# Attention blocks of a fused attention and two-layer MLP kernel: the values of one block and the scores of the next issued as one run of TensorE into two shared PSUM banks

## The chip, the cores and the metric

The kernel runs on one core of a Trainium2 chip. The metric is the device time of one execution in microseconds (us). The kernel before took 1147.94 us in the median of three runs (1147.36 to 1148.22). The profile is of one further execution.

## What is computed

The reference has three parts in a chain. The first is chunked attention: every chunk of 32 queries sees 8 memory keys, 16 tokens to the left, its own 32 and 8 to the right, 64 keys in the middle of a sequence. The other two are MLP layers on 3072 tokens, with a model width of 512 and a hidden width of 2048.

```python
# attention: batch 4, 8 heads, 768 tokens, head size 64; for every chunk of 32 queries
k_full = concatenate([mem_k, k_ctx], axis=2)
scores = scale * matmul(q_c, k_full.transpose(0, 1, 3, 2))
scores = scores - max(scores, axis=-1, keepdims=True)
a = exp(scores)
a = a / (sum(a, axis=-1, keepdims=True) + 1e-09)
out[:, :, c_start:c_end] = matmul(a, v_full)
# layer 1
h = x @ w_in
x = maximum(0.01 * h, h) @ w_out
# layer 2
h = x @ w_in2
P = a[0] + a[1]*h + a[2]*h**2 + a[3]*h**3
Q = 1 + abs(b[0])*abs(h) + abs(b[1])*h**2
out = (P / (Q + 1e-6)) @ w_out2
```

## The kernel before

The MLP layers are cut into 6 tiles of 512 tokens, and each tile into 16 steps `c` over the hidden width. A step has 12 matmuls of 128x512 for the hidden values (`emit_h`, PSUM tile `hps`) and 12 for the sum over the hidden width (`emit_y` in layer 1, `emit_o` in layer 2, PSUM tiles `acc`). `emit_h` runs two steps ahead in layer 1. Between the two groups of a step, and behind the second, there are gaps, numbered 2c and 2c+1, in which other work is put; `wide(slot)` calls what the table `wide_at` holds for that gap. Gaps are places in the program's order and not times: each engine works through its own list and waits for semaphores.

Attention for the first two tiles is computed before, in small ("narrow") blocks. For the other four tiles it is computed in 16 "wide" blocks of 128 tokens, numbered 8 to 23, while the matmuls of layer 1 run. `wide_plan` says in which gap each part of block j stands. Its scores stand in gap u = at[j], which is 28, 35 and 42 for blocks 8 to 10, 49 for block 11, and 8 more for each later block. The parts are:

- `wide_load_qk`, `wide_load_v`: loads of q and k by SyncE's DMA queue (SP), of v by GpSimd's (POOL).
- `wide_q`, `wide_k` (VectorE): transposes of 32x32 pieces, then a write to a DRAM buffer (`park_dram`); `wide_qk` reads that back with rows and columns rearranged. A block thus turns its q (tile `qT`) and k (tile `pb`) by a trip through DRAM.
- `wide_s`: the scores, 32 matmuls on 64x32 pieces of the array (64 rows, 32 columns) into two PSUM banks (tile `pss`), then on VectorE the row maximum and its subtraction (lines 634 and 635), which move the scores to the SBUF tile `t`.
- `wide_e` (ScalarE): exp. `wide_n` (VectorE): sum, reciprocal, product.
- `wide_p` (VectorE): transposes to tile `pm`, then a write to DRAM (line 546); `turn_in(2, ...)` reads it back in four parts (line 553).
- `wide_x`: the values, 32 matmuls on 64x64 pieces into two more PSUM banks (tile `psx`), then a copy on ScalarE (line 675) and a subtraction on VectorE (line 676) that make the two parts of the layer's input.

The pool `psw` has four PSUM banks, shared in turn by `hps`, `pss` and `psx`. `stage` puts the preparation of layer 2's weights into the same gaps: a load of 512 KB (line 227), a ScalarE scaling, three VectorE operations (lines 246 to 249) and a store (line 272). SyncE's queue issues its DMAs in program order, so a DMA that waits for its data holds up those behind it. An fp32 matmul of the small kind stands in the trace as two.

Of the kernel before, what the change touches and what calls it, by code (L numbers as in the profile page):

```python
# [9 lines left out]
F32 = mybir.dt.float32  # L10
# [6 lines left out]
P = 128  # L17
# [7 lines left out]
def kernel(  # L25
# [507 lines left out]
    PW = WIN // 2  # L533
    MP = NM // 2
    WPS = S // P
    wq, wqT, wm = {}, {}, {}
    v_mem, k_mem = [None], [None]
    kw = kall.rearrange("p n h d -> p (n h d)")
    kwT = pall.rearrange("p n c e h m -> p (n c e h m)")
    vw = vall.rearrange("p n h d -> p (n h d)").rearrange("p (c h d) -> p c h d", c=NCH, h=H // 2)  # L540
# [7 lines left out]
    def turn_in(n, j, dst):  # L548

        d = dst.rearrange("p (c w) -> p c w", c=NCH)  # L550
        s = park[n][j % 2].rearrange("(c p) (g w) -> g p c w", c=NCH, g=4)
        for g in range(4):
            nc.sync.dma_start(out=d[g * 32:(g + 1) * 32], in_=s[g])
# [57 lines left out]
    def wide_qk(j):  # L611
        turn_in(0, j, wqT[j])
        turn_in(1, j, kwT)

    def wide_s(j):
        blk = j % WPS
        qt = wqT.pop(j).rearrange("p (c n m) -> p c n m", c=NCH, n=NP)
        kt = kwT.rearrange("p (c n m) -> p c n m", c=NCH, n=NP)
        ps = [psw.tile([P, 512], F32, tag="ps", name="pss")[:, :NP * WIN].rearrange("p (n m) -> p n m", n=NP)
              for e in range(2)]  # L620
        for p in range(NP):
            for e in range(2):
                r = slice(e * 64, e * 64 + 64)
                for c in range(NCH):
                    nc.tensor.matmul(ps[e][c * CHUNK:(c + 1) * CHUNK, p, :], qt[r, c, p, :], kt[r, c, p, :],  # L625
                                     start=True, stop=True)
        mx = tmp.tile([P, 2, NP, 1], F32, tag="mx", name="mx")
        t = tmp.tile([P, 2, NP, WIN], F32, tag="P", name="t", bufs=3)
        for e in range(2):
            if blk == 0:  # L630
                nc.vector.memset(ps[e][0:CHUNK, :, NM:NM + LCTX], NEG)
            if blk == WPS - 1:
                nc.vector.memset(ps[e][P - CHUNK:P, :, WIN - RCTX:WIN], NEG)
            nc.vector.tensor_reduce(out=mx[:, e], in_=ps[e], op=ALU.max, axis=AX.X, negate=True)
            nc.vector.tensor_tensor(out=t[:, e], in0=ps[e], in1=mx[:, e].to_broadcast([P, NP, WIN]), op=ALU.add)
        wm[j] = t
# [20 lines left out]

    def wide_x(j):
        pt = pwT.rearrange("p (c h m) -> p c h m", c=NCH, h=4)
        ps = [psw.tile([P, 512], F32, tag="ps", name="psx")[:, :2 * P].rearrange("p (i m) -> p i m", i=2)  # L660
              for hh in range(2)]
        for i in range(2):
            for c in range(NCH):
                for hh in range(2):
                    r = slice(hh * WIN, hh * WIN + WIN)
                    for e in range(2):
                        nc.tensor.matmul(ps[hh][e * 64:e * 64 + 64, i, c * CHUNK:(c + 1) * CHUNK],  # L667
                                         vw[r, c, 2 * i + e, :], pt[r, c, 2 * i + e, :], start=True, stop=True)
        n, o = divmod(j * P, NMAX)
        if n not in xt:  # L670
            xt[n] = (xpool.tile([P, KC, NMAX], F32R, tag="xh", name="xh"),
                     xpool.tile([P, KC, NMAX], F32R, tag="xl", name="xl"))
        for hh in range(2):
            xh, xl = (x[:, 2 * hh:2 * hh + 2, o:o + P] for x in xt[n])
            nc.scalar.copy(out=xh, in_=ps[hh])
            nc.vector.tensor_tensor(out=xl, in0=ps[hh], in1=xh.bitcast(F32), op=ALU.subtract)
# [5 lines left out]
    def wide_plan():  # L682
        def put(slot, *fns):
            wide_at.setdefault(slot, []).extend(fns)
        n0 = WIDE_FROM * NMAX // P
        last = NT // P - 1
        TB = NMAX // P
        base = 2 * FC * (WIDE_FROM - 1)
        at = {j: base - 7 + 8 * (j - n0) for j in range(n0, last + 1)}
        at[n0], at[n0 + 1], at[n0 + 2] = base - 4, base + 3, base + 10  # L690
        put(at[n0] - 7, lambda: wide_load_qk(n0))
        put(at[n0] - 5, lambda: wide_q(n0), lambda: wide_k(n0))
        put(at[n0] - 4, lambda: wide_qk(n0), lambda: wide_load_qk(n0 + 1))
        for j in range(n0, last + 1):
            u = at[j]
            put(u, lambda j=j: wide_s(j))
            put(u + 1, lambda j=j: wide_e(j))
            if j < last:
                put(u + 1, lambda j=j: wide_q(j + 1))
                put(u + 2, lambda j=j: wide_k(j + 1))  # L700
                put(u + 3, lambda j=j: wide_qk(j + 1))
            put(u + 3, lambda j=j: wide_n(j), lambda j=j: wide_load_v(j))
            put(u + 4, lambda j=j: wide_p(j))
            put(u + 5, lambda j=j: turn_in(2, j, pwT))
            put(u + 6, lambda j=j: wide_load_qk(j + 2))
            put(u + (9 if j % TB == TB - 1 else 10), lambda j=j: wide_x(j))

    def wide(slot):
        for fn in wide_at.get(slot, ()):
# [383 lines left out]
```

## Time and profile before

| | |
|---|---|
| median of three runs | 1147.94 us |
| profiled execution, its time | 1148.0 us |
| its span, first to last instruction | 1146.2 us |
| TensorE matmul busy | 1131.7 us (99%) |
| VectorE, ScalarE, GpSimd busy | 67%, 55%, 20% |
| chain that ended last | TensorE 95%, VectorE 3% |
| wide values and wide scores, share of that chain | 2% and 1% |
| TensorE's waits from 136 to 530 us, where the wide blocks are | 0.4 us |

The span begins with the first instruction and ends with the last; the 1.8 us between it and the profiled execution's time lie outside. Busy time of TensorE is the union of its matmul records, which overlap since matmuls are pipelined: a record of a 128x512 matmul lasts 0.39 us, and the next begins 0.23 us after it. Costs on TensorE are therefore read from starts, not from durations. In the rows of a timeline equal instructions that follow each other are merged, with their number at the end, and a bracket gives idle time and who ended it. A row of the DMA queue of SyncE (SPq) says when DMAs were issued and not when they landed.

### The profile page before, as it was taken

The page shows a single profiled execution, that of the slowest core. Times are in us where ns is not written, and L with a number is a line of the kernel's source. Part 1 is how long each engine was busy: PE and PEld are TensorE (multiplying, and loading weights), DVE is VectorE, ACT ScalarE, POOL GpSimd, SP SyncE. Part 2 cuts the span into 40 slices and gives each one's busy share as a digit, 9 for nine tenths or more (in the row PEclk, how much of TensorE's full clock was granted, in tenths as well). Part 3 has the DMA queues.
Part 4 walks back from the last instruction along what each step waited for, and adds up shares of the span by engine and source line. Part 5 has one row for each costly group of instructions (what it writes and reads, how often), then busy time and mean ns, then how long its engine had stood idle before and what let it go on. Part 6 is the DMA issues. An engine that isn't in the chain of part 4 may idle for free.

```text
span 1146.2 us, 19651 instructions
## 1 busy us (share of the span) xinstructions
PE 1131.7 (99%) x7616; PEld 928.3 (81%) x7616; DVE 769.7 (67%) x1318; ACT 631.8 (55%) x1149; POOL 232.1 (20%) x264
## 2 busy tenths in 40 slices
PE   7999999999999999999999999999999999999998
PEld 6777788888888888888888888888888888888886
DVE  5887846555565555542345886887887888788775
ACT  4677632232232223223346876776777777777765
POOL 3000302231221322210000222222222222222222
PEclk9999999999999999999999999999999999999999
DMA  9966687797778777742342101001100100100101
GB/s 187 260 178 196 187 226 206 213 251 206 202 215 241 208 196 230 207 142 98 97 133 83 65 1 47 28 1 39 36 1 29 46 1 15 59 1 1 37 1 37
DMA packets 148472, 131.98 MB, mean 115 GB/s; under 512 B 63296, under 2 KB 118944, under 8 KB 148380
## 3 DMA queue, kind: packets, MB, share of 16 engines
q1 hardware_dynamic: 143372, 123.25, 37.6%
q0 software_dynamic: 4864, 7.45, 2.8%
q8 instruction: 60, 0.98, 0.4%
q14 instruction: 32, 0.26, 0.1%
q10 hardware_dynamic: 144, 0.03, 0.0%
HBM read 92.92 MB, written 37.75 MB: 114 GB/s over the span
## 4 chain that ended last, share of the span: by engine, by line
PE 95%; DVE 3%; ACT 1%; issue 1%; POOL 0%; DVEq 0%; POOLq 0%
PE hps L753 45%; PE acc L849 23%; PE acc L811 22%; PE psx L667 2%; PE pss L625 1%; PE pss L460 1%; PE hot L867 1%; DVE wwall L178 1%; PE psx L444 0%; PE psx L514 0%; DVE wwall L180 0%; PE psk L378 0%; DVE wwall L177 0%; ACT w L188 0%; DVE w L194 0%
## 5 line engine op out<-in xcount | busy, mean ns | idle before, releaser
L811 PE MATMUL acc<-g,w 128*128 128x512 f32 x1152 | 278.7, 391 | 0.1
L849 PE MATMUL acc<-w,g 128*128 128x512 f32 x1152 | 275.4, 389 | 0.0
L849 PEld LDWEIGHTS acc<-w,g 128*128 128x128 f32 x1152 | 216.2, 188 | 44.8
L811 PEld LDWEIGHTS acc<-g,w 128*128 128x128 f32 x1152 | 214.7, 188 | 46.1 <-ACT w L188 0.5
L763 ACT ACTIVATE g<-hps 128x512 fp32r<-128x512 f32 x96 | 57.4, 598 | 307.1 <-PE hps L753 307.1
L789 POOL TENSOR_TENSOR g<-R,g 128x512 fp32r<-128x512 f32 x96 | 124.2, 1294 | 504.4 <-ACT g L788 466.1
L753 PE MATMUL hps<-xh,w 128*128 128x512 f32 x768 | 209.0, 395 | 3.8 <-ACT pm L484 1.5
L753 PE MATMUL hps<-yh,w 128*128 128x512 f32 x768 | 204.1, 389 | 0.0
L766 DVE TENSOR_TENSOR g<-s,g 128x512 fp32r<-128x512 f32 x96 | 66.2, 690 | 177.6 <-ACT s L764 174.4
L753 PEld LDWEIGHTS hps<-xh,w 128*128 128x128 f32 x768 | 141.2, 188 | 34.6 <-ACT w L188 2.0
L753 PEld LDWEIGHTS hps<-yh,w 128*128 128x128 f32 x768 | 144.3, 188 | 29.9
L590 POOL DMA_DIRECT2D vb<-in_v_dram x128 | 83.2, 651 | 260.5 <-PE psx L667 207.9
L776 ACT ACTIVATE A<-hps 128x512 f32<-128x512 f32 x96 | 57.2, 596 | 113.9 <-PE hps L753 113.9
L792 DVE SCALAR_TENSOR_TENSOR A<-A,small,pb 128x512 f32<-128x512 f32 x96 | 72.0, 750 | 56.2 <-ACT pb L777 56.2
L753 PE MATMUL hps<-xl,w 128*128 128x512 f32 x384 | 103.0, 390 | 0.0
L753 PE MATMUL hps<-yl,w 128*128 128x512 f32 x384 | 102.6, 389 | 0.0
L783 DVE SCALAR_TENSOR_TENSOR A<-A,pb 128x512 f32<-128x512 f32 x96 | 66.5, 692 | 30.2 <-ACT pb L796 30.2
L753 PEld LDWEIGHTS hps<-xl,w 128*128 128x128 f32 x384 | 72.1, 188 | 15.7
L753 PEld LDWEIGHTS hps<-yl,w 128*128 128x128 f32 x384 | 72.1, 188 | 14.9
L778 ACT ACTIVATE R<-hps,small 128x512 f32<-128x512 f32 x96 | 75.0, 781 | 0.0
L785 DVE SCALAR_TENSOR_TENSOR R<-R,small,A 128x512 f32<-128x512 f32 x96 | 72.2, 752 | 3.4
L794 DVE SCALAR_TENSOR_TENSOR R<-R,small,hps 128x512 f32<-128x512 f32 x96 | 71.8, 748 | 3.4
(112 smaller groups left out, 1140.1 us busy)
## 6 DMA issues: line engine op xcount, KB each, us to landing
wr<-in_moe_w_in_dram SPq DMA_DIRECT2D x32, 512.0 KB
wr<-in_moe_w_out_dram SPq DMA_DIRECT2D x32, 512.0 KB
park_dram<-pb SPq DMA_DIRECT2D x16, 512.0 KB
pb<-park_dram SPq DMA_DIRECT2D x64, 128.0 KB
w_dram<-wwall SPq DMA_DIRECT2D x32, 256.0 KB
wb<-w_dram SPq DMA_DIRECT2D x32, 256.0 KB
kb<-in_k_dram SPq DMA_DIRECT2D x59, 112.0 KB
vb<-in_v_dram POOLq DMA_DIRECT2D x118, 56.0 KB, 3.3
```

The costliest lines, as they stand in the source:

```text
L590: nc.gpsimd.dma_start(out=vw[r + at:r + at + n, c], in_=v[bi, hs, lo:lo + n, :].rearrange("h p d -> p h d"))
L753: nc.tensor.matmul(ps[:, :n], w_[:, ws], x_[:, kk, :], start=(kk == 0 and m == 0), stop=(kk == KC - 1 and m == 2))
L763: nc.scalar.activation(out=gh, in_=ps, func=AF.Prelu, alpha=0.01)
L766: return [lambda: nc.vector.tensor_tensor(out=gl, in0=s, in1=gh.bitcast(F32), op=ALU.subtract)]
L778: nc.scalar.activation(out=R, in_=ps, func=AF.Identity, scale=ncf[:, 3:4], bias=ncf[:, 2:3])
L783: nc.vector.scalar_tensor_tensor(out=A0, in0=A0, scalar=ONE, in1=U0, op0=ALU.add, op1=ALU.mult)
L785: nc.vector.scalar_tensor_tensor(out=R0, in0=R0, scalar=ncf[:, 0:1], in1=A0, op0=ALU.add, op1=ALU.mult)
L789: nc.gpsimd.tensor_tensor(out=gl, in0=R0, in1=gh.bitcast(F32), op=ALU.subtract)
L792: nc.vector.scalar_tensor_tensor(out=A, in0=A, scalar=babs[:, 1:2], in1=U, op0=ALU.mult, op1=ALU.add)
L794: nc.vector.scalar_tensor_tensor(out=R, in0=R, scalar=ncf[:, 1:2], in1=ps, op0=ALU.add, op1=ALU.mult)
L811: nc.tensor.matmul(acc[i][d][:, :n], w_[:, ws], g_, start=(f == 0 and m == 0), stop=(f == FC - 1 and m == 2))
L849: nc.tensor.matmul(acc[i][s], g_[:, ss], w_, start=(f == 0 and m == 0), stop=(f == FC - 1 and m == 2))
```

## The change

Values of block j-1 and scores of block j are issued in one gap, u of block j: first the 32 value matmuls, then the 32 score matmuls, then VectorE's maximum and subtraction of the scores (now a function of its own, `wide_m`), and then the copy and subtraction of the values (`wide_y`). Both write to the same two PSUM banks, taken by `wide_banks` for the whole run: the scores to columns 0 to 255 of a bank, the values to columns 256 to 511. Values of block j thus stand in gap u+8 (u+7 for blocks 8 to 10), where they stood in u+10 or u+9. Normalisation, transposes with their write to DRAM, and the read back move up by a gap each, from u+3, u+4 and u+5 to u+2, u+3 and u+4, and the load of v from u+3 to u+2.

```diff
+    def wide_banks():
+        banks[:] = [psw.tile([P, 512], F32, tag="ps", name="run") for _ in range(2)]
+
     def wide_s(j):
         ...
-        ps = [psw.tile([P, 512], F32, tag="ps", name="pss")[:, :NP * WIN].rearrange("p (n m) -> p n m", n=NP)
-              for e in range(2)]
+        ps = [t[:, :NP * WIN].rearrange("p (n m) -> p n m", n=NP) for t in banks]
         ...
+        wm[j] = ps
+
+    def wide_m(j):
+        blk = j % WPS
+        ps = wm[j]
         ...
     def wide_x(j):
         pt = pwT.rearrange("p (c h m) -> p c h m", c=NCH, h=4)
-        ps = [psw.tile([P, 512], F32, tag="ps", name="psx")[:, :2 * P].rearrange("p (i m) -> p i m", i=2)
-              for hh in range(2)]
+        ps = [t[:, 512 - 2 * P:].rearrange("p (i m) -> p i m", i=2) for t in banks]
         ...
+        wx[j] = ps
+
+    def wide_y(j):
+        ps = wx.pop(j)
         ...
             u = at[j]
-            put(u, lambda j=j: wide_s(j))
+            if j > n0:
+                put(u, wide_banks, lambda j=j: wide_x(j - 1), lambda j=j: wide_s(j),
+                    lambda j=j: wide_m(j), lambda j=j: wide_y(j - 1))
+            else:
+                put(u, wide_banks, lambda j=j: wide_s(j), lambda j=j: wide_m(j))
             put(u + 1, lambda j=j: wide_e(j))
             ...
-            put(u + 3, lambda j=j: wide_n(j), lambda j=j: wide_load_v(j))
-            put(u + 4, lambda j=j: wide_p(j))
-            put(u + 5, lambda j=j: turn_in(2, j, pwT))
+            put(u + 2, lambda j=j: wide_n(j), lambda j=j: wide_load_v(j))
+            put(u + 3, lambda j=j: wide_p(j))
+            put(u + 4, lambda j=j: turn_in(2, j, pwT))
             put(u + 6, lambda j=j: wide_load_qk(j + 2))
-            put(u + (9 if j % TB == TB - 1 else 10), lambda j=j: wide_x(j))
+        put(at[last] + 8, wide_banks, lambda: wide_x(last), lambda: wide_y(last))
```

TensorE before, from the last matmuls ahead of the scores of block 10 to behind the values of block 9. The scores are line 625 and the values line 667.

```order
L753 MATMUL hps<-xh,w 128x512 x4
L625 MATMUL pss<-pb,qT 32x64 x32
L811 MATMUL acc<-g,w 128x512 x12
L753 MATMUL hps<-xh,w 128x512 x4
L753 MATMUL hps<-xl,w 128x512 x4
L753 MATMUL hps<-xh,w 128x512 x4
L811 MATMUL acc<-g,w 128x512 x12
L667 MATMUL psx<-pm,vb 64x32 x32
L753 MATMUL hps<-xh,w 128x512 x4
```

TensorE now, at the same place. Lines 674 and 628 are the values and the scores, 768 and 826 are what 753 and 811 were.

```order
L768 MATMUL hps<-xh,w 128x512 x4
L674 MATMUL run<-pm,vb 64x32 x32
L628 MATMUL run<-pb,qT 32x64 x32
L826 MATMUL acc<-g,w 128x512 x12
L768 MATMUL hps<-xh,w 128x512 x4
L768 MATMUL hps<-xl,w 128x512 x4
L768 MATMUL hps<-xh,w 128x512 x4
L826 MATMUL acc<-g,w 128x512 x12
L768 MATMUL hps<-xh,w 128x512 x4
```

The values of block 9 moved from 36 big matmuls behind the scores of block 10 to directly ahead of them.

VectorE before, in the same block 10, from the transposes of k of block 11 (line 608) to the transposes to `pm` (line 655); line 676 belongs to the values of block 9, lines 644 to 647 are the normalisation, 246 to 249 the weights.

```order
L608 STREAM_TRANSPOSE pb<-kb 128x4x2x32 x4
L676 TENSOR_TENSOR xl<-psx,xh 128x2x128 x2
L644 TENSOR_REDUCE sm<-t 128x8
L645 TENSOR_SCALAR sm<-sm 128x8
L646 RECIPROCAL sm<-sm 128x8
L647 TENSOR_TENSOR t<-t,sm 128x512
L246 TENSOR_SCALAR wwall<-wwall 128x512
L247 SCALAR_TENSOR_TENSOR wwall<-wr,wwall 128x512
L249 SCALAR_TENSOR_TENSOR wwall<-wr,wwall 128x512
L766 TENSOR_TENSOR g<-s,g 128x512
L655 STREAM_TRANSPOSE pm<-t 128x2x2x32 x4
```

VectorE now, at that place (609, 652 to 655 and 663 are what 608, 644 to 647 and 655 were).

```order
L609 STREAM_TRANSPOSE pb<-kb 128x4x2x32 x4
L652 TENSOR_REDUCE sm<-t 128x8
L653 TENSOR_SCALAR sm<-sm 128x8
L654 RECIPROCAL sm<-sm 128x8
L655 TENSOR_TENSOR t<-t,sm 128x512
L663 STREAM_TRANSPOSE pm<-t 128x2x2x32 x4
L246 TENSOR_SCALAR wwall<-wwall 128x512
```

The subtraction of the values is gone from here, and the transposes to `pm` stand ahead of the weights' operations and of one `g`.

SyncE's DMA queue before, block 10: the trip of q and k of block 11 and of `pm` of block 10 through DRAM.

```order
L546 DMA park_dram<-pb 128x1024
L553 DMA qT<-park_dram 32x4x128 x4
L553 DMA pb<-park_dram 32x4x256 x4
L227 DMA wr<-in_moe_w_out_dram 128x1024
L546 DMA park_dram<-pm 128x512
L272 DMA w_dram<-wwall 128x512
L553 DMA pm<-park_dram 32x4x128 x4
```

The same place of the queue now.

```order
L547 DMA park_dram<-pb 128x1024
L554 DMA qT<-park_dram 32x4x128 x4
L554 DMA pb<-park_dram 32x4x256 x4
L547 DMA park_dram<-pm 128x512
L227 DMA wr<-in_moe_w_out_dram 128x1024
L554 DMA pm<-park_dram 32x4x128 x4
L272 DMA w_dram<-wwall 128x512
```

The write of `pm` went ahead of the 512 KB load, and its read back ahead of the weights' store.

## Rows read from the trace of the kernel before

**Rows 1.** Busy time 136 to 530 us: length, engines (count), granted clock, DMA share, GB/s.
```profile
136.00:530.00 394.00, 393.64 (x3618) 320.20 (x3617) 214.35 (x489) 117.74 (x228) 87.83 (x138) 1.00 0.74 206
```

**Rows 2.** Chain of waits, its last long piece: start us, length us, what.
```profile
1131.24 10.89 PE acc L849 x48
```

**Rows 3.** Timeline of TensorE, 182 to 199 us: start us, length us, instruction, count.
```profile
185.89 0.86 PE L625 MATMUL pss<-pb,qT 64*32 64x64 f32 x64
186.68 3.02 PE L811 MATMUL acc<-g,w 128*128 128x512 f32 x12
...
192.25 2.88 PE L811 MATMUL acc<-g,w 128*128 128x512 f32 x12
195.07 1.14 PE L667 MATMUL psx<-pm,vb 64*64 64x32 f32 x64
```

**Rows 4.** Groups by line and shape: count, busy us, mean ns, idle before.
```profile
L625 PE MATMUL pss<-pb,qT 64*32 64x64 f32 x1024 | 13.9, 224 | 0.0
```

**Rows 5.** Timeline of TensorE, narrow blocks, 70 and 119 us.
```profile
70.92 0.38 PE L502 MATMUL pst<-ident,pm 128*128 128x128 f32 x2
71.24 0.65 PE L460 MATMUL pss<-kT,qT 64*32 64x64 f32 x32
...
119.16 0.38 PE L502 MATMUL pst<-ident,pm 128*128 128x128 f32 x2
119.30 3.01 PE L811 MATMUL acc<-g,w 128*128 128x512 f32 x12
```

**Rows 6.** Timeline of TensorE: scores of blocks 8, 9, 11, 12 and 13.
```profile
144.07 1.00 PE L625 MATMUL pss<-pb,qT 64*32 64x64 f32 x64
...
164.27 0.86 PE L625 MATMUL pss<-pb,qT 64*32 64x64 f32 x64
...
207.24 0.86 PE L625 MATMUL pss<-pb,qT 64*32 64x64 f32 x64
...
231.31 0.86 PE L625 MATMUL pss<-pb,qT 64*32 64x64 f32 x64
...
255.37 0.86 PE L625 MATMUL pss<-pb,qT 64*32 64x64 f32 x64
```

**Rows 7.** Timeline of SyncE's DMA queue (issues), block 8.
```profile
156.47 1.80 SPq L553 DMA_DIRECT2D pb<-park_dram  x4
158.85 0.69 SPq L546 DMA_DIRECT2D park_dram<-pm  x1
161.95 1.73 SPq L553 DMA_DIRECT2D pm<-park_dram  x4
```

**Rows 8.** The same queue, block 9.
```profile
176.91 3.58 SPq L553 DMA_DIRECT2D pb<-park_dram  x4
...
181.10 0.38 SPq L546 DMA_DIRECT2D park_dram<-pm  x1
185.31 1.74 SPq L553 DMA_DIRECT2D pm<-park_dram  x4
```

**Rows 9.** The same queue, block 10.
```profile
195.88 0.32 SPq L546 DMA_DIRECT2D park_dram<-pb  x1
...
201.05 1.73 SPq L553 DMA_DIRECT2D pb<-park_dram  x4
...
203.36 0.38 SPq L546 DMA_DIRECT2D park_dram<-pm  x1
...
209.72 1.82 SPq L553 DMA_DIRECT2D pm<-park_dram  x4
```

**Rows 10.** The same queue, block 13.
```profile
274.48 1.75 SPq L553 DMA_DIRECT2D pm<-park_dram  x4
```

**Rows 11.** The same queue, block 23, when little else is moved.
```profile
511.64 0.32 SPq L546 DMA_DIRECT2D park_dram<-pm  x1
...
513.74 1.74 SPq L553 DMA_DIRECT2D pm<-park_dram  x4
```

**Rows 12.** DMA issues: count, KB each, median us from issue to landing.
```profile
vb<-in_v_dram POOLq DMA_DIRECT2D x118, 56.0 KB, 3.3
```

More of the change, by code (lines that the diff above doesn't have):

```diff
@@ L535 @@
     WPS = S // P
-    wq, wqT, wm = {}, {}, {}
+    wq, wqT, wm, wx = {}, {}, {}, {}
     v_mem, k_mem = [None], [None]
+    banks = []
     kw = kall.rearrange("p n h d -> p (n h d)")
```

## The prediction

> **What bounds the kernel now.** I read the busy time by stretch first: from 136 to 530 us, where all wide blocks stand, TensorE's matmuls cover 393.64 of 394 us at the full granted clock, while VectorE is busy for 214 us of them [rows 1]. So in this stretch TensorE's own list is the time. A change there can win only by making that list shorter, and loses as soon as TensorE has to wait, since there is no slack to take it up. Next I read the price of a small run from TensorE's timeline, and last the DMA queue of SyncE, because the values need `pm`, which comes back from DRAM.
>
> **The joined run.** Big matmuls follow each other every 10.89/48 = 0.227 us [rows 2]. What a separate small run costs beyond its own matmuls has three parts. At its start: from 192.25 to 195.07 us are 2.82 us, 12 steps of 0.227 are 2.72, so 0.10 are lost [rows 3]. At its end: the scores' row of 0.86 us from 185.89 includes the last matmul of 0.22 [rows 4], which thus starts at 186.53, and the next big one at 186.68: 0.15. Behind it the 12 big matmuls take 3.02 in place of 2.88 us: 0.14 [rows 3]. Together 0.39 us. The change joins 15 pairs (values of block 23 stay alone), so 15 starts and ends go, and 15 turns from values to scores inside a run come in.
>
> No row shows that turn. The nearest is in the narrow blocks, where transposes are followed at once by scores: 0.32 us from the first of one to the first of the other, against 0.14 where the same transposes are followed by a big matmul [rows 5]. That turn costs 0.18 us. If the new turn is free the gain is 15 x 0.39 = 5.8 us; if it costs as much as an end and a start, nothing. I take 0.18, the nearest row: 15 x 0.21 = 3.1 us gained. The Trainium skill has a rule on this, TensorEngine Tiling (Array Packing), Key Properties: changing the tiling mode, and not merely the tile, drains TensorE. Values use 64x64 pieces and scores 64x32, so by that rule a drain stays in each joined run and the gain is the 3.1 us; without it, the 5.8 us. The pair in [rows 5] agrees with the rule, and no run here shows the new pair.
>
> The 64 value and 64 score records themselves are the same, with the same waits for loads and reads.
>
> **What else moves at no price.** ScalarE's copies of the values now wait for VectorE's two operations per bank on the scores, since both read the same bank; that is up to 1.7 us (four operations of 0.42), and the next ScalarE work behind them waits for 12 big matmuls (2.7 us) anyway. Banks: a run takes two of four for its whole length, but only once per block where it was twice, and the next `hps` that needs one of them is issued several us later. The load of v starts when the previous values are done, as before, and has the same eight gaps. VectorE and ScalarE do the same operations in another order.
>
> **The values come sooner: does `pm` come soon enough?** The values of block j now stand ahead of the scores of j+1. So I measure from the start of the scores of j to the start of that run, with the value run that used to lie between taken out (1.14 - 0.22 + 0.39 = 1.3 us [rows 3, 4]), and compare with the arrival of `pm`. The arrival is the end of the row of its read plus a landing. A write and its read back show 2.1 us in a quiet queue [rows 11], loads of v of nearly the size of one part 3.3 us [rows 12], both from the issue; the last part is issued some 0.4 us before its row ends, so 1.7 to 2.9 us after the row's end. I take 2.0, nearer to the row of the same queue.
>
> Block 8: 164.27 - 144.07 = 20.2 us are available [rows 6], no value run lay between. The read's row ends at 163.68 [rows 7]. The write at 158.85 can move up to the end of the row ahead, 158.27, so 0.6 earlier: arrival 165.1, 0.8 us late.
>
> Block 9: 185.89 - 164.27 - 1.3 = 20.3 us [rows 3, 6]. The read's row ended 22.8 us behind the scores [rows 8]; with landing 24.8, thus 4.5 late if nothing moved. It moves: the weights' store now stands behind the write, and VectorE's k no longer stands behind the subtraction of values. The four reads of k, stretched to 3.58 us by a wait for a 512 KB load eight DMAs ahead, stay. I take 2 us of gain: 2.5 late.
>
> Block 10: 207.24 - 185.89 - 1.3 = 20.05 us [rows 3, 6]. The read's row ends at 211.54, with landing 27.65 behind the scores, 7.6 late if nothing moved [rows 9]. VectorE's part ends much sooner in the new order, but the write of `pm` still stands behind the read of k, and that one waits for k's write (195.88 to 201.05). The read of k ends at 202.78, so the write gains 0.6. It now goes ahead of the 512 KB load; its trip took 6.4 us, block 9's 4.2 [rows 8, 9]: 2.2 gained. For k's own trip, 5.2 us, I allow 1.0, since loads of v start earlier. Together 3.8: also 3.8 late.
>
> Blocks 11 to 22: 24.06 - 1.3 = 22.8 us are available [rows 6]. In block 13 the read's row ends 20.9 us behind the scores, with landing 22.9 [rows 10]: level if nothing moved. Here normalisation and transposes come up by a gap and the big matmuls that VectorE's list waits for by the 1.3 us of the moved value run, so 1.5 us or more are gained: no wait.
>
> TensorE waits 0.8 + 2.5 + 3.8 = 7.1 us, and gains 3.1: 4.0 us slower. The profiled execution took 1148.0 us (its span of 1146.2 and 1.8 around it), the median is 1147.94, so nothing is corrected: **1152 us**.
>
> Bounds: the waits are 2 us if trips take what block 8's took (3.1 us, [rows 7]) and reads land in 1.7; 13 if nothing moves (1.4, 4.5 and 7.6, rounded). The gain is 0 to 5.8. That is 1144 to 1161.
>
> **Rivals.**
> - *Faster: `pm` arrives in time.* The block's trip has two writes and two reads in a row on one queue. The mechanism is traffic: loads of v start a few us earlier and the 512 KB load goes behind the write; if trips in blocks 9 and 10 fall to about 2.1 us [rows 11], block 10 gains 3.1 us on k's write and 4.3 on `pm`'s, 8.0 with the 0.6 above, more than the 7.6 it lacked; block 9 likewise. Then the gain stands alone: 1142.2 to 1144.9. It decides where the waits sum to under 0.8 us with the turn as taken, or under 3.5 with a free turn. Against it: the DMA engines are busy to 0.74 in this stretch [rows 1]. The Trainium skill speaks for it, DMA: Bandwidth & Descriptors, Anatomy of one DMA: a fixed cost of about 2.0 us and bytes over 436 GB/s, an estimate of 2.6 us for 256 KB, on GpSimd's path. The trace shows 2.1 in block 23 and 4.2 to 6.4 in blocks 9 and 10, so it disagrees where it matters.
> - *No change.* Waits of 2 to 5 us against a gain of about the same: 1146 to 1150.
> - *Much slower.* TensorE stands still for up to 4 us, and no row of this stretch shows such a wait, so none shows what the granted clock does behind it. If it fell to the lower of its two levels for as long as each wait of over 2 us lasted, the big matmuls of those 6.3 us would take twice as long, an estimate of 3 us more: 1155. The same comes out if the turn eats the whole gain (1148 + 7.1): the change would then not do what it says.
>
> **How the numbers follow.** Forecast (waits outweigh the gain by 2.3 us or more) 0.43 and much slower 0.12; no change 0.25; in time, faster 0.20. 0.2% is 2.3 us, about what a measurement can tell from no change here. So slower 0.55, same 0.25, faster 0.20. The likeliest case alone gives 1150.3 to 1154; the range for 8 in 10 reaches into both sides, 1144.5 to 1157.
>
> **What would show it.** Right: the timeline of TensorE has waits of 0.5 to 4 us ahead of the values of blocks 8, 9 and 10, ended by the read of `pm`, and none of note behind; between values and scores about 0.2 us. Wrong: the first value matmul of block 10 follows its big matmul after 0.3 us, with a busy share of 99% and over: then the arrival was mis-sized. Waits in blocks 13 to 22 would show that a gap less is too little everywhere, and a time above 1157 that I missed a cost.

## The result and the profile after

The changed kernel takes 1157.91 us (median of 4 runs, 1157.21 to 1160.65) where the kernel before took 1148.08 on the same chip: a ratio of 1.0091, 95% interval 1.0073 to 1.0109. It is slower, as forecast, but by 9.8 us and not by 4, and 0.9 us beyond the upper end of the range. The profiled execution took 1157.21 us, its span is 1155.4; that is 9.2 us more than the profiled execution of before (1148.0).

Line numbers have moved: scores are L628 now, values L674, `hps` L768, `acc` L826 and L864, the write of `pm` L547 and its read L554. First the stretch of the wide blocks by windows (columns as in [rows 1]), then what TensorE waited for in it.

```profile
136.00:540.00 404.00, 395.47 (x3623) 324.79 (x3622) 211.86 (x490) 119.66 (x230) 88.16 (x139) 1.00 0.75 201
```

```profile
PE run L674 <- DMA pm<-park_dram: 5.3, 8, 1.4
PE hps L768 <- issue: 2.7, 1, 2.7
PE hps L768 <- DVE w L194: 0.4, 1, 0.4
```

TensorE, which was covered but for 0.36 us [rows 1], now stands for 8.5 us. Of this 5.3 us are eight waits of the values for `pm`, and one wait of 2.7 us, marked "issue" (nothing that the profile shows was waited for), is of a kind that the prediction did not have. TensorE's timeline of three joined runs shows the first kind: values of block 8, of block 9, and of block 11, the first that waits for nothing. Columns: start us, length us, instruction, count, idle time before it and what ended it.

```profile
163.71 0.84 PE L826 MATMUL acc<-g,w 128*128 128x512 f32 x3
164.90 0.30 PE L674 MATMUL run<-pm,vb 64*64 64x32 f32 x4 [0.34 <-DMA pm<-park_dram]
165.87 1.62 PE L674 MATMUL run<-pm,vb 64*64 64x32 f32 x60 [0.67 <-DMA pm<-park_dram]
167.42 0.86 PE L628 MATMUL run<-pb,qT 64*32 64x64 f32 x64
168.20 0.97 PE L768 MATMUL hps<-xh,w 128*128 128x512 f32 x3
...
186.70 0.84 PE L768 MATMUL hps<-xh,w 128*128 128x512 f32 x3
188.92 0.30 PE L674 MATMUL run<-pm,vb 64*64 64x32 f32 x4 [1.38 <-DMA pm<-park_dram]
189.87 1.12 PE L674 MATMUL run<-pm,vb 64*64 64x32 f32 x60 [0.64 <-DMA pm<-park_dram]
190.92 0.86 PE L628 MATMUL run<-pb,qT 64*32 64x64 f32 x64
191.71 0.50 PE L826 MATMUL acc<-g,w 128*128 128x512 f32 x1
...
235.33 0.84 PE L826 MATMUL acc<-g,w 128*128 128x512 f32 x3
236.11 1.13 PE L674 MATMUL run<-pm,vb 64*64 64x32 f32 x64
237.17 0.86 PE L628 MATMUL run<-pb,qT 64*32 64x64 f32 x64
237.96 1.20 PE L768 MATMUL hps<-xh,w 128*128 128x512 f32 x4
```

From the three big matmuls ahead to the first big one behind are 2.63 us in the clean run of block 11, 4.49 at block 8 and 5.01 at block 9: the waits cost 1.86 and 2.38 us there. The same difference is 1.29 at block 10 and, where the prediction had none, 0.23, 0.47, 0.31, 0.15 and 1.68 at blocks 12, 13, 17, 18 and 21: 8.4 us in all. This is more than the 5.3 us that the waits list, since the values also run slower where their inputs trickle in: block 8's last 60 take 1.62 us where all 64 of block 11 take 1.13. Not all of it is waiting for `pm`. The values of blocks 8, 12 and 18 take 0.27, 0.27 and 0.21 us longer than the others in the kernel before too, and those of 12 and 18 are as slow (0.28 and 0.15) in e2 below, which does not read `pm`. So behind block 10 the waits for `pm` are those of blocks 13, 17 and 21, 2.5 us, and against the kernel before the 8.4 us are 7.6.

The second kind stands behind the joined run of block 17. TensorE's timeline, and then the windows over it (length, TensorE busy, granted clock, DMA share, GB/s):

```profile
383.17 0.39 PE L768 MATMUL hps<-xl,w 128*128 128x512 f32 x1
386.21 1.01 PE L768 MATMUL hps<-xl,w 128*128 128x512 f32 x3 [2.66 <-issue]
```

```profile
383.50:386.20 2.70, 0.05 (x1) 1.00 1.18 208
...
387.00:390.40 3.40, 3.40 (x9) 0.50 0.67 153
```

TensorE stops in the middle of a group of big matmuls, with nothing that the profile shows to wait for, and soon after it goes on the granted clock is 0.50 (1.2 of 2.4 GHz) for 3.4 us, which costs half of that, 1.7 us.

### The profile page after: what moved, and what is told of

Same layout as the page of the kernel before. It is cut to its first block, busy times and chain, and to the rows that moved or that the text cites. A ratio compares the mean times of both kernels' runs of the same rounds, so it can differ in the third digit from the quotient of the medians.

```text
span 1155.4 us, 19656 instructions
## 1 busy us (share of the span) xinstructions
PE 1132.8 (98%) x7616; PEld 931.9 (81%) x7616; DVE 766.7 (66%) x1318; ACT 633.2 (55%) x1149; POOL 232.1 (20%) x264
## 4 chain that ended last, share of the span: by engine, by line
PE 88%; DMA 4%; DVE 3%; SPq 2%; ACT 1%; issue 1%; DVEq 0%
PE hps L768 42%; PE acc L864 23%; PE acc L826 19%; PE run L674 1%; DMA park_dram<-pm 1%; PE run L628 1%; DMA pm<-park_dram 1%; PE pss L460 1%; DMA qT<-park_dram 1%; SPq L554 1%; DMA qr<-in_q_dram 1%; DMA w_dram<-wwall 0%; PE psx L444 0%; DMA vb<-in_v_dram 0%; PE psx L514 0%
## 5 line engine op out<-in xcount | busy, mean ns | idle before, releaser
L826 PE MATMUL acc<-g,w 128*128 128x512 f32 x1152 | 278.7, 391 | 0.0
L864 PE MATMUL acc<-w,g 128*128 128x512 f32 x1152 | 275.4, 389 | 0.0
L826 PEld LDWEIGHTS acc<-g,w 128*128 128x128 f32 x1152 | 215.9, 188 | 46.5 <-ACT w L188 0.5
L864 PEld LDWEIGHTS acc<-w,g 128*128 128x128 f32 x1152 | 216.2, 188 | 44.9
L768 PE MATMUL hps<-xh,w 128*128 128x512 f32 x768 | 209.0, 395 | 3.8 <-ACT pm L484 1.5
L768 PE MATMUL hps<-yh,w 128*128 128x512 f32 x768 | 204.1, 389 | 0.0
L768 PEld LDWEIGHTS hps<-xh,w 128*128 128x128 f32 x768 | 142.3, 188 | 35.3 <-ACT w L188 2.0
L768 PEld LDWEIGHTS hps<-yh,w 128*128 128x128 f32 x768 | 144.1, 188 | 29.9
L768 PE MATMUL hps<-xl,w 128*128 128x512 f32 x384 | 103.2, 390 | 2.7 <-issue 2.7
L768 PE MATMUL hps<-yl,w 128*128 128x512 f32 x384 | 102.6, 389 | 0.0
L768 PEld LDWEIGHTS hps<-xl,w 128*128 128x128 f32 x384 | 72.0, 188 | 18.5 <-issue 3.1
L768 PEld LDWEIGHTS hps<-yl,w 128*128 128x128 f32 x384 | 72.1, 188 | 15.0
```

The lines of the kernel that those rows point to most:

```text
L768: nc.tensor.matmul(ps[:, :n], w_[:, ws], x_[:, kk, :], start=(kk == 0 and m == 0), stop=(kk == KC - 1 and m == 2))
L826: nc.tensor.matmul(acc[i][d][:, :n], w_[:, ws], g_, start=(f == 0 and m == 0), stop=(f == FC - 1 and m == 2))
L864: nc.tensor.matmul(acc[i][s], g_[:, ss], w_, start=(f == 0 and m == 0), stop=(f == FC - 1 and m == 2))
```

## The experiments

Twelve runs, in three groups that each share the kernel before: 1148.24 us, 1148.56 and 1148.80 (medians).

### The normalisation alone (e1)

The kernel before, with normalisation, transposes and the trip of `pm` a gap earlier; nothing joined, and the load of v where it was.
```
-            put(u + 3, lambda j=j: wide_n(j), lambda j=j: wide_load_v(j))
-            put(u + 4, lambda j=j: wide_p(j))
-            put(u + 5, lambda j=j: turn_in(2, j, pwT))
+            put(u + 2, lambda j=j: wide_n(j))
+            put(u + 3, lambda j=j: wide_load_v(j))
+            put(u + 3, lambda j=j: wide_p(j))
+            put(u + 4, lambda j=j: turn_in(2, j, pwT))
```


> The kernel before with one part of the change alone: normalisation, the transposes to pm with their write, and the read back stand a gap earlier; scores and values stay in their own runs and gaps. Theory A (TensorE waits for pm because the values stand two gaps sooner): nothing is late here, the time is that of the kernel before, 1148 us within 1. Rival C (the new order on VectorE and on the DMA queue holds up the big matmuls): a good part of the 9.8 us shows, 1151 or more.

Measured: 1148.12 us (10 runs, 1147.70 to 1148.39), ratio 1.000, interval 0.999 to 1.0009; no wait of TensorE but the 0.4 us for a weight. Nothing is gained or lost by the earlier normalisation itself.

### Values that don't wait for `pm` (e2, twice as e12)

The changed kernel with values that read the identity in place of `pm`; the attention weights are thus left out of the result.
```
-        pt = pwT.rearrange("p (c h m) -> p c h m", c=NCH, h=4)
+        pt = ident.rearrange("p (h m) -> p h m", h=4)
...
```


> The changed kernel, whose values read the identity matrix in place of pm, so that they wait for v alone; pm is still computed, written and read back, and the attention weights are left out of the result. Theory A: the waits for pm, 8.4 us in the changed profile, go and the joined runs' gain of 3.3 us stays: 1145 to 1146.5 us if the instruction wait of 2.7 us and the clock's fall came with the waits. Rival B (a joined run of 128 small matmuls starves TensorE of instructions, and the clock falls behind that, whatever pm does): about 1149.5 to 1151.

> The kernel without the wait for pm once more, unchanged (values read the identity; attention weights left out of the result), for its spread and for the place of its stalls in a second profile. By theory J a stall marked as issue stands at a joined run, at a place that need not be that of the first profile (block 12), and a fetch on the instruction queue starts in the joined run or behind it rather than ahead of it; the runs spread over 4 us or more again. By the rival that the spread was an accident of that one session they lie within 1.5 us.

Measured: 1147.81 us (10 runs, 1144.62 to 1151.76), ratio 0.9998, interval 0.9983 to 1.0013; again, 1149.10 (1145.61 to 1151.04), ratio 1.0000, interval 0.9989 to 1.0010. Both lie between what A and B forecast. Without the waits for `pm` the changed kernel's time falls by some 10 us, to that of the kernel before. The best run lies 3.6 us under the median of the kernel before, about the whole gain of joining, but the median shows none, and runs of one kernel lie 5 to 7 us apart. What eats the gain is on TensorE's timeline, here of the first of the two runs:

```profile
254.67 1.42 PE L674 MATMUL run<-ident,vb 64*64 64x32 f32 x64
256.02 0.83 PE L628 MATMUL run<-pb,qT 64*32 64x64 f32 x58
258.38 0.31 PE L628 MATMUL run<-pb,qT 64*32 64x64 f32 x6 [1.52 <-issue]
```

The scores stop after the 58th of 64, in the middle of a run whose operands have arrived, with a wait for "issue". In the second run it is the same joined run (values of block 12) and the same place, behind the 58th score, for 3.17 us.

### `pm` ahead of q and k in the queue (e3)

```
-            put(u + 2, lambda j=j: wide_n(j), lambda j=j: wide_load_v(j))
-            put(u + 3, lambda j=j: wide_p(j))
+            put(u + 2, lambda j=j: wide_n(j), lambda j=j: wide_p(j), lambda j=j: wide_load_v(j))
```


> The changed kernel with the transposes to pm and their write one gap earlier still, right behind the normalisation, so that the write of pm stands ahead of the reads of q and k in the DMA queue of SyncE. Theory A, in the form that pm is late because its trip stands behind that of k in one queue: the write leaves some 2 to 4 us sooner, the waits fall from 8.4 us to 2 or less, 1149 to 1152 us. If traffic and not the order makes pm late, or the reads of q and k become late in its place: 1156 or more. Rival B: no change but the waits' part, so a wait for instructions stays.

Measured: 1154.4 us (4 runs, 1152.13 to 1158.08), ratio 1.0058, interval 1.0036 to 1.0080. TensorE's longest waits in the wide blocks:

```profile
PE run L674 <- DMA pm<-park_dram: 3.5, 3, 2.2
PE run L628 <- issue: 0.9, 1, 0.9
```

Three waits for `pm` are left, two at block 9 (1.11 and 0.18 us) and one at block 10 (2.22); blocks 12 to 22 have none. There the lateness was the place of `pm`'s write in SyncE's queue, behind the reads of q and k. Blocks 9 and 10 stay late, so the forecast of 1149 to 1152 us and 2 us of waits is missed; the profiled execution is the fastest of the four, and what the others lose more isn't seen. Behind the wait of block 10 the granted clock is 0.57 on average from 211 to 215 us, so a wait for `pm` can bring the clock down too.

### Blocks 8 to 10 apart (e4)

```
-            if j > n0:
+            if j > n0 + 3:
...
+            put(u + (2 if j > n0 + 3 else 3), lambda j=j: wide_load_v(j))
...
+            if j < n0 + 3:
+                put(u + 10, wide_banks, lambda j=j: wide_x(j), lambda j=j: wide_y(j))
```


> The changed kernel with the values of blocks 8, 9 and 10 back in a run of their own, ten gaps behind their scores; joined are the runs from block 12's scores on (12 in place of 15). Theory A: the waits ahead of the values of blocks 8 to 10 (5.5 us in the changed profile) go and three joinings at 0.22 us are lost: about 1153 us. Rival B: the loss is spread over the joined runs, so 3 of 15 of it go: about 1156 us.

Measured: 1153.5 us (5 runs, 1152.35 to 1157.22), ratio 1.0043, interval 1.0029 to 1.0057.

```profile
PE run L674 <- DMA pm<-park_dram: 4.0, 6, 0.9
PE hps L771 <- issue: 3.9, 1, 3.9
```

Without the three blocks at the short distance the time falls by 4.4 us, near the 4.9 that these blocks' waits less their joins come to (1.86 + 2.38 + 1.29 - 3 x 0.22); the late blocks still wait, and a wait for issue of 3.9 us comes in behind the joined run of block 17, with another of 0.6 elsewhere. These rows are of the slowest of the five executions (1157.22 us), and in it block 11, which waited for nothing in the changed kernel, waits too (0.49 and 0.78 us). So that 4.4 comes near 4.9 does not show that nothing else changed.

### Values in a run of their own (e5)

As e2 (attention weights left out), but values and scores stand apart, in neighbouring gaps.
```
-            if j > n0:
-                put(u, wide_banks, lambda j=j: wide_x(j - 1), lambda j=j: wide_s(j),
-                    lambda j=j: wide_m(j), lambda j=j: wide_y(j - 1))
-            else:
-                put(u, wide_banks, lambda j=j: wide_s(j), lambda j=j: wide_m(j))
+            put(u, wide_banks, lambda j=j: wide_s(j), lambda j=j: wide_m(j))
...
+                put(at[j + 1] - 1, wide_banks, lambda j=j: wide_x(j), lambda j=j: wide_y(j))
```


> The changed kernel with the values taken out of the joined run: they stand in a run of their own in the gap before the scores of the next block (two gaps or so earlier than in the kernel before), and read the identity in place of pm, so they wait for no transfer; the attention weights are left out of the result. The normalisation, the trip of pm and the v loads stay as early as in the changed kernel. Theory F: the spread of the kernel without the wait for pm (1144.6 to 1151.8 us) and its stalls marked as issue belong to the joining: 128 small matmuls and their weight loads in 1.7 us use up TensorE's instructions faster than a late fetch on the instruction queue brings new ones. Then this kernel shows no issue stall ahead of or behind a small run, its runs lie within 1.5 us of one another, and its time is that of the kernel before, 1148.1 +- 0.5 us. Rival G: the stalls come from what else the change moved (earlier normalisation, trip and v loads, earlier copies of the values). Then the runs spread by 4 us or more, and a stall of 1.5 us or more marked as issue stands in the window of the wide blocks.

Measured: 1148.57 us (10 runs, 1148.14 to 1150.28), ratio 1.0003, interval 0.9993 to 1.0012; TensorE's only wait in the wide blocks is the 0.4 us for a weight. The runs lie 2.1 us apart, a little over the 1.5 that theory F allowed, but within what the kernel before showed beside them (1147.76 to 1150.72). Joined or not is the difference to e2, so the waits for issue come from the joining, as F said.

### A longer joined run (e6)

As e2 (attention weights left out), with each matmul of the values issued twice: 192 small ones in a run.
```
-        for i in range(2):
+        for i in (0, 0, 1, 1):
```


> The kernel without the wait for pm (values read the identity, attention weights left out of the result), with every matmul of the values issued twice in the joined run: 192 small matmuls instead of 128. The 64 more cost 0.86 to 1.06 us a run by the clean joined run of the changed kernel (values to scores 1.06 us, scores to the next big matmul 0.86 to 1.0), 13 to 16 us in 15 runs. Theory F (late fetch of instructions): a longer run empties TensorE's instructions more often, so issue stalls of 1.5 to 4 us stand in a third of the 15 runs or more, and the time is above the 1144.6 + 16 = 1160.6 us of the best run without stalls: 1165 us or more, with issue waits of 8 us or more in all in the profile. Rival G (the stall is an accident of the place or of the clock, whatever the length of the run): 1158 to 1163 us, issue waits of 2 us or less.

Measured: 1199.62 us (4 runs, 1197.67 to 1201.00), ratio 1.0436, interval 1.0415 to 1.0456: 52 us over e2 where the matmuls themselves are 13 to 16.

```profile
PE run L628 <- issue: 23.4, 7, 5.0
PE run L674 <- issue: 3.1, 1, 3.1
PE hps L768 <- issue: 1.3, 1, 1.3
PE acc L826 <- issue: 0.9, 1, 0.9
```

Ten waits of 28.7 us in all stand where the run with 128 had one of 1.5. The mean granted clock from 136 to 590 us is 0.96, some 36 us at half speed, which costs up to 18 us more. A longer run brings the waits, as theory F has it, and far beyond its 8 us.

### The trip of `pm` made early enough (e7, twice as e11)

The changed kernel with blocks 8 to 11 apart as before, `pm` turned and written a gap earlier from block 12 on, and loads of q and k, from those of block 13 on, a gap earlier, ahead of the stores of y. The load of v stays in gap u+3 up to block 12.
```
-            if j > n0:
+            if j > n0 + 4:
...
+            put(u + (2 if j > n0 + 4 else 3), lambda j=j: wide_load_v(j))
+            put(u + (2 if j > n0 + 3 else 3), lambda j=j: wide_p(j))
...
+            put(u + (5 if j > n0 + 2 else 6), lambda j=j: wide_load_qk(j + 2))
+            if j < n0 + 4:
+                put(u + (10 if j < n0 + 3 else 9), wide_banks, lambda j=j: wide_x(j), lambda j=j: wide_y(j))
```


> The changed kernel with what the waits for pm point at undone: blocks 8 to 11 keep values and scores apart as before (joined from block 12's values on, 11 joins), from block 12 on pm is turned and written a gap earlier, and the loads of q and k for block after next are issued a gap earlier, ahead of the stores of y in SP's queue. Theory A (the waits for pm are a matter of when its trip is issued): waits for pm of 1 us or less in all, and of the 11 joins 11 x 0.22 = 2.4 us are gained: 1145.7 us without any issue stall, 1148 with stalls as large as in the kernel without the wait for pm (3.2 us in 15 runs, 2.3 in 11). Rival B (the transfers themselves are slow beside the others, however early they are issued): pm waits of 2 us or more stay in blocks 13, 17 or 21, and the time is 1150 us or more.

> The kernel with the early trip once more, unchanged, for its spread and its distance to the kernel before on the same chip: 1145.9 us within 1.5 us over all runs if its eleven joins bring no stall, and 2.5 us under the kernel before.

Measured: 1145.88 us (8 runs, 1145.22 to 1146.70), ratio 0.9975, interval 0.9964 to 0.9986; again, 1146.15 (11 runs, 1145.66 to 1147.14), ratio 0.9974, interval 0.9965 to 0.9983. This kernel beats both the one before (by 2.7 us) and the changed one (by 12). TensorE waits for nothing but the weight, and the joined run of block 21, the latest behind block 10 in the changed kernel, is as the clean one above:

```profile
470.90 1.14 PE L674 MATMUL run<-pm,vb 64*64 64x32 f32 x64
471.96 0.86 PE L628 MATMUL run<-pb,qT 64*32 64x64 f32 x64
472.75 1.20 PE L771 MATMUL hps<-xh,w 128*128 128x512 f32 x4
```

2.7 us are 0.24 for each of 11 joins. Theory A is right: late is where the trip was issued, not how fast the transfers are. Whether the earlier loads of q and k were needed beside the earlier write wasn't tried apart; e3 had no late block from 12 on without them.

### Scores ahead of the values in the joined run (e8)

```
-                put(u, wide_banks, lambda j=j: wide_x(j - 1), lambda j=j: wide_s(j),
+                put(u, wide_banks, lambda j=j: wide_s(j), lambda j=j: wide_x(j - 1),
```


> The changed kernel with one thing turned: within the joined run the scores of the next block stand ahead of the values of this one, so pm has some 0.9 us longer (the scores' own time in the joined run, 0.86 us). Theory A (each wait for pm is lateness on TensorE's path, and nothing else): the waits of 1.87, 2.39, 1.29, 0.23, 0.47, 0.31, 0.15 and 1.69 us shrink by 0.9 each, to 3.7 us in all, so the time falls by 4.7 us to 1153.2 us; issue stalls stay as they were. Rival C (the turn from scores to values costs more than that from values to scores, or VectorE, which now gets the values later, binds the run's banks): less than 2 us are gained, 1156 to 1158 us, with a turn above 0.3 us inside the run or a wait for VectorE behind it.

Measured: 1155.13 us (4 runs, 1154.33 to 1156.38), ratio 1.0055, interval 1.0039 to 1.0071: 2.8 us better than the changed kernel, 4.7 expected. The listed waits shrink to three:

```profile
PE run L674 <- DMA pm<-park_dram: 3.0, 3, 1.7
```

The wait for issue of the changed kernel's profile and the clock fall behind it (2.7 and 1.7 us) are not in this one, though the forecast kept them. Two costs stand against that. Behind the two waits of block 9 (0.78 and 1.72 us) the granted clock is 0.50 for 6.8 us, from 190.0 on, which costs 3.4 us (columns as in [rows 1]):

```profile
189.00:192.50 3.50, 2.40 (x61) 2.32 (x62) 0.59 (x2) 0.00 (x0) 0.89 (x2) 0.64 0.83 187
192.50:196.00 3.50, 3.50 (x10) 2.69 (x9) 2.45 (x7) 1.27 (x3) 1.05 (x2) 0.50 1.03 283
```

And by the starts of single matmuls, a joined run without a wait takes 1.71 us from its first to its last matmul with values first and 1.80 with scores first, so 15 turns cost 1.4 us more. The profiled executions differ by 2.6 us, which leaves some 3 us (2.6 - 2.7 - 1.7 + 3.4 + 1.4) by which the lateness of `pm` shrank, not 4.7. So A has the sign right and the size too large. C falls as it was put: more than 2 us are gained, and the turn is 0.24 us, 0.15 to the first value and 0.09 more among the values, under its 0.3.

### Which joins carry the waits for issue (e9, e10)

e9 is e2 with e7's order of transfers and all 15 joins; e10 joins only the values of blocks 8 to 11 with the scores behind them. Both read the identity as e2 does (attention weights left out).
```
 e10, on e9:
-            if j > n0:
+            if n0 < j <= n0 + 4:
...
+            if n0 + 4 <= j < last:
+                put(at[j + 1] - 1, wide_banks, lambda j=j: wide_x(j), lambda j=j: wide_y(j))
```


> The kernel without the wait for pm (values read the identity; attention weights left out of the result), all 15 joins as in the changed kernel, with the order of transfers of the kernel with the early trip: loads of q and k a gap earlier, from block 12 on pm written a gap earlier. Theory J (the stalls marked as issue go with the joins themselves, above all the four of blocks 8 to 11, which the kernel with the early trip keeps apart and which lie beside the heaviest traffic): runs spread over 4 us or more as they did without the early order (1144.6 to 1151.8), median 1147 to 1149. Theory O (the order of transfers decides whether a fetch of instructions is late): with the early order the runs lie within 1.5 us, at 1148.5 less 15 x 0.22 = 1145.2 us.

> As the run with all 15 joins and the early order, but joined only where the values of blocks 8 to 11 meet the scores of blocks 9 to 12; from block 12 on values have a run of their own in the gap before the next scores (values read the identity; attention weights left out of the result). Theory J (the first four joins carry the stalls): spread of 4 us or more, median 1148 to 1151. Theory O (order of transfers): within 1.5 us, at 1148.5 less 4 x 0.22 = 1147.6 us.

Measured: e9 1150.64 us (10 runs, 1145.52 to 1152.57), ratio 1.0004, interval 0.9990 to 1.0018; e10 1149.64 (10 runs, 1148.44 to 1150.38), ratio 1.0005, interval 0.9996 to 1.0014. With all joins the spread of 7 us is back, whatever the order of transfers, so theory O falls. But the first four joins alone bring no wait for issue in the profile and a spread of 1.9 us, so the part of J that blames them is not borne out; the join at which e2, e12 and e9 stop, with the values of block 12, is the fifth. That profile is of one of the faster executions (1148.67 us), and where the 0.9 us of gain went isn't settled. In e9 the wait stands once more behind the 58th score of block 12's joined run:

```profile
256.04 0.83 PE L628 MATMUL run<-pb,qT 64*32 64x64 f32 x58
260.55 0.43 PE L628 MATMUL run<-pb,qT 64*32 64x64 f32 x6 [3.68 <-issue]
```

Behind it the granted clock is 0.50 for 6.8 us, in e12 for 3.4, and in e2, whose wait was 1.52 us, it stays at 1.00. Half of that is lost. Added to the waits and to 1145.2 us (1148.5 less 3.3 for 15 joins), this gives 1146.7, 1150.1 and 1152.3 us for e2, e12 and e9; their profiled executions took 1146.91, 1149.38 and 1152.57. So where a profile shows it, the spread is the wait and the clock behind it.

Three executions of two kernels that stop at the same instruction point to the supply of instructions. The DMA queues show it (queue and kind: packets, MB, share of the window), first of e9 from 237 us to within the stop (to 257.9) and from there to 260.5, when TensorE goes on:

```profile
q1 hardware_dynamic: 4919, 4.45, 80.7%
q0 software_dynamic: 436, 0.43, 9.6%
...
q1 hardware_dynamic: 586, 0.82, 88.9%
...
q8 instruction: 1, 0.02, 2.4%
```

And of e7 from 238 us to 255.4, just ahead of the same joined run (255.8):

```profile
q1 hardware_dynamic: 4475, 3.95, 86.7%
...
q8 instruction: 1, 0.02, 0.5%
```

In e7 a packet of 16 KB on the instruction queue came ahead of the run (at 251.0 us), and nothing waits. In e9 none came for 21 us; the next starts at 258.25, takes 1.0, and TensorE goes on 1.3 us after its end. In e2 and e12 the packets start at 256.04 and 257.04 us and TensorE goes on at 258.38 and 259.47. The changed kernel has the same at block 17: no packet on queue 8 from 361 to 383.5 us, one at 383.62, and TensorE goes on at 386.21. Twenty us without a packet are no cause by themselves: in the changed kernel none starts between 389.00 and 413.31 us, over the joined run of block 18, and nothing waits there for issue.

A count shows what TensorE stops at. Take all of its records in a trace from the start on: matmuls, weight loads and the few semaphore instructions. Ahead of the instruction that ends a wait for issue, in the changed kernel, e2, e3, e4, e6, e9 and e12, stand 256k + 193 or 256k + 194 records, in all 17 cases, and k is each time the number of packets that had landed on queue 8. TensorE goes on 1.3 to 1.7 us after the end of the last of them. So the stops lie on a grid of 256 records, as many as there are for one packet of 16 KB (15,436 for 60 in the changed kernel), and TensorE goes on only when the next packet has landed.

## Why the prediction was right or wrong

**What bounds the kernel** was right: every stand of TensorE comes back in the time. The profiled executions differ by 9.2 us; waits for `pm` of 7.6, issue of 2.7 and 1.7 for the clock, less a gain of 3.3, are 8.7, and 0.3 had been lost before the scores of block 8 (at 144.36 for 144.07 [rows 6]).

**The joined run's gain** was right: 3.1 us forecast. By the starts of single matmuls, with the slower big ones behind included, a clean joined run costs 2.09 us, a run of scores alone 1.02 and one of values alone 1.29, so 0.22 are gained by each join, 3.3 by 15. The turn from the last of the values to the first score is 0.15 us (0.18 taken from [rows 5]); e7 shows the gain by itself. The Trainium skill's rule that a change of tiling mode drains TensorE (TensorEngine Tiling (Array Packing), Key Properties) agrees with that: the turn is ten times the 0.0145 us between two values, and joining does not take it away.

**Blocks 8 to 10** were right in mechanism and their sum roughly so: 5.5 us (1.86, 2.38 and 1.29) for 7.1. The parts were not: block 8 waits over twice the 0.8 forecast, block 10 a third of the 3.8. (The lower bound of 2 us was loose as well: trips of 3.1 us and landings in 1.7 make about 3 by the same steps.) SyncE's queue in the changed kernel at block 10:

```profile
203.69 1.73 SPq L554 DMA_DIRECT2D pb<-park_dram  x4
205.52 0.38 SPq L547 DMA_DIRECT2D park_dram<-pm  x1
...
208.49 1.74 SPq L554 DMA_DIRECT2D pm<-park_dram  x4
```

Its scores start at 190.92, so the write stands 14.6 us behind them where it stood 17.5 [rows 3, 9]: 2.9 gained for 1.6 forecast. From write to read are 3.0 us where there were 6.4: 3.4 for 2.2. At block 9 the 2 us of gain came as taken. At block 8 the write did not move up by 0.6 us: the read of k ahead of it took 2.82 us, not 1.80 [rows 7].

**The step that failed** is "Blocks 11 to 22: ... no wait": 2.5 us of waits stand there, at blocks 13, 17 and 21. I measured one block, 13, found it level, and took the gap that normalisation comes up as gained by all; but the write of `pm` stands in the queue behind the reads of q and k, and so does not come up with VectorE. Block 13 in the changed kernel, its scores and the read of its `pm`:

```profile
261.26 0.86 PE L628 MATMUL run<-pb,qT 64*32 64x64 f32 x64
...
281.04 1.73 SPq L554 DMA_DIRECT2D pm<-park_dram  x4
```

The read's row ends 21.5 us behind the scores where it ended 20.9 [rows 6, 10]: 0.6 us later, not 1.5 sooner. The three blocks lie alike, behind the end of a tile, and the worst is block 21. SyncE's queue there:

```profile
454.14 3.17 SPq L832 DMA_DIRECT2D y_dram<-wwall  x4
...
469.86 0.32 SPq L547 DMA_DIRECT2D park_dram<-pb  x1
470.32 2.17 SPq L554 DMA_DIRECT2D qT<-park_dram  x4
472.74 3.13 SPq L554 DMA_DIRECT2D pb<-park_dram  x4
475.96 0.38 SPq L547 DMA_DIRECT2D park_dram<-pm  x1
478.68 1.73 SPq L554 DMA_DIRECT2D pm<-park_dram  x4
```

Four stores of y stand ahead of the loads of q and k for block 22 (as others do, at 258.29 and 354.32 us, ahead of those for blocks 14 and 18); k's write comes at 469.86, the write of block 21's `pm` stands behind both reads at 475.96, and its read ends at 480.41, just as TensorE arrives. e3 and e7, in which `pm` goes first, have no such wait.

**A second step failed, and cost more**: the sentence that the 128 small records "are the same, with the same waits", at no price. They are the same, but 128 matmuls and as many weight loads in 1.7 us ask for instructions faster than a late packet brings them: 2.7 us here, and 1.7 for the clock fall behind it, 4.4 together. The fall itself stood among the rivals, as "much slower", behind the waits for `pm`; in this execution it came behind the wait for issue, in e3 and e8 behind waits for `pm`. The median lies 0.7 us over the profiled execution, and e2 lies 10 us under it where the waits for `pm` come to some 8; these differences stay open.

The Trainium skill has a rule on the supply (Runtime: NRT & Kernel Launch, Instruction fetch mechanics): instructions come in blocks of 16 KiB, 256 instructions, and the fetch is hidden, since a sequencer needs some 20 cycles for each. The first half agrees: one packet of 16 KB comes for about each 128 matmuls with their loads, and all 17 waits end on a grid of 256 records. The second does not hold in a joined run, where 256 instructions start in 1.71 us, 6.7 ns each, and the runs show waits of 0.6 to 5.0 us.

What decides whether a packet is late is open: kernels with the same code near the stop (e7, e9) differ in it. That it is a matter of supply is shown by the place of all 17 stops, the packets ahead of which TensorE does not go on, and the length (e5, e6); no run changed the supply itself.

## What to carry to other kernels

When a consumer is moved ahead, follow its transfer through the queue for each kind of block, those behind a tile's end too: an engine that finishes earlier gains nothing if its DMA stands behind one that waits for something else. Where TensorE has no slack, joining short runs is worth only the boundaries (here 0.22 us each) and is to be done only where the inputs have time to spare; 11 joins with time to spare gained 2.7 us, 15 with waits lost 9.8. Long rows of small matmuls have a price of their own, so look in the trace for idle time marked "issue" and for the instruction queue's packets beside it.

## What the runs showed of the hardware

Runs of 128 small matmuls stopped TensorE for 0.6 to 3.9 us for want of instructions, three times at the same one, and runs of 192 in ten waits of 0.6 to 5.0 us, always on the grid of 256 records, and until 1.3 to 1.7 us after the end of the next packet of 16 KB. The profiles of e7, e8, e10 and e11 have runs of 128 and no such wait, and the kernels with separate runs of 64 (before, e1, e5) showed none among the wide blocks. Turning from 64x64 to 64x32 pieces costs 0.15 us, back 0.24.

The granted clock was 0.50 for 3.4 us behind the stand of 2.66 us in the changed kernel, and for 6.8 behind that of 3.68 in e9; behind 1.52 us in e2 it stayed at 1.00. Behind two waits of block 9 it stayed at 1.00 in the changed kernel (1.38 and 0.64 us) and was 0.50 for 6.8 us in e8 (0.78 and 1.72).
